# Closing waits for unawaited transfers only, and the last output chunk in two column parts

## The chip, the cores and the metric

The kernel runs on one core of a Trainium2 chip. The metric is the device time in microseconds of one execution. A profile gives the span from the first to the last instruction; in every execution of this study the time is 1.8 to 1.9 us longer than the span, whatever the kernel.

## The reference

Linear attention with a per-head RMS norm, then a residual token-mixing layer and a two-layer MLP on 8 batches of 576 x 512. Only the last lines matter here:

```python
u  = x + lam * tok
a2 = alpha2 * u + beta2
ch = np.maximum(a2 @ w_ch1, 0.0) @ w_ch2
return (u + lam * ch).astype(np.float32)
```

## The kernel before

A small scheduler in the kernel file places operations on engines and works out the waits between them. In the program a semaphore is a counter that an engine or a transfer (DMA) raises and on which another engine waits. Each DMA has a semaphore of its own; at the end SyncE waits for every one.

```python
    def emit(self):
        ...
        for o in self.sequence:
            if o.lat is not None:                      # a DMA
                val[o.idx] = (self.stack.enter_context(nc.semaphore("d%d" % o.idx)), 16)
            elif o.inc:
                count[o.eng] += 1
                val[o.idx] = (sems[o.eng], count[o.eng])
        ...
            for o in self.sequence:
                ...                                    # waits, the operation, its increment
            for o in self.sequence:
                if o.lat is not None:
                    nc.sync.wait_ge(*val[o.idx])       # the closing waits
```

The second MLP layer of batch `b` handles chunks of 128 rows in the order 0 to 4 (four in even batches). Chunk 4 holds the last 64 rows of two batches, so it needs two stores of 64 rows.

```python
        def ch2(b, pri, span):
            ...
            nch = 5 if b % 2 else 4
            def mm(c, fj, p):
                ...                                     # 16 matmuls of 128x512 into t
                P.op({"DVE": dve_us(512)}, lambda e, _: e.tensor_tensor(
                    out=lc[:], in0=t.flat(), in1=lam_bc[:], op=ALU.mult), ...)
                P.op(..., lambda e, _: e.tensor_tensor(out=x, in0=x, in1=lc[:], op=ALU.add), ...)
                if c < 4:
                    ... e.dma_start(out[b, c:512:4, :], x)
                else:
                    for i in range(2):
                        ... e.dma_start(out[b - 1 + i, 512:576, :], x[64 * i:64 * i + 64, :])
            order = ... [(c, fj) for c in range(nch) for fj in range(16)]
```

## Time and profile before

| quantity | value |
|---|---|
| time, median of the first 3 runs | 367.05 us (365.95 to 367.85) |
| span of the profiled run | 365.81 us |
| PE busy | 354.1 us (97%) |
| PE's end to the end of the span | 7.44 us |
| of that: closing waits of SyncE | 68 instructions, 361.01 to 365.49 us |

SP or SyncE is the engine that issues the stores and the closing waits (SPq in the views), DVE the vector engine, PEld PE's weight loads. First the page's rows over 40 equal slices of the span (tenths busy; PEclk is PE's granted clock):

```profile
PE   8999999999899999999999999999999999999991
PEclk9899999999999999999999999999999999999997
```

PE is busy for over 80% of every slice but the last. The chain of waits of the last 25 us (start, duration, what) shows why:

```profile
341.14 10.74 PE ps L1046 x49
351.88 0.05 issue
351.93 6.44 PE ps L1046 x29
358.37 0.02 issue
358.39 0.70 DVE lc L1054
359.09 0.02 issue
359.12 0.69 DVE xtl L1059
```

PE runs without a hole to 358.37. Then DVE multiplies and adds the last chunk. The timeline of the same stretch goes on to the two stores (each line's two figures are start and extent):

```profile
358.39 0.69 DVE L1054 TENSOR_TENSOR lc<-ps,lam_bc 128x512 f32<-128x512 f32 x1 [2.04 <-PE ps L1046]
359.12 0.69 DVE L1059 TENSOR_TENSOR xtl<-xtl,lc 128x512 f32<-128x512 f32 x1
359.84 1.12 SPq L1066 DMA_DIRECT2D out_dram<-xtl  x2
```

The stores are issued by 360.96, yet the span lasts to 365.81. Waits are not listed in the timeline; the view by source line has them. First the line of the closing waits (duration of one, then first and last start):

```profile
L403 SPq EVENT_SEMAPHORE  x68: 28/28/28, 361.0 to 365.5; - x68
```

Each is listed at 28 ns, but in the trace their starts stand 61 ns apart (the median; the last one starts 0.38 us after the one before), so 68 of them fill 4.5 us. (Each waits for two semaphores: the builder had paired the 136 waits.) A table by stage shows that nothing else happens in most of that time (columns: stretch, its length, busy time of PE, PEld, DVE, ACT, POOL, then PEclk, DMA share, GB/s):

```profile
358.40:359.84 1.44, 0.00 (x0) 0.00 (x0) 1.38 (x2) 0.00 (x0) 0.00 (x0) 1.00 0.00 0
359.84:361.00 1.16, 0.00 (x0) 0.00 (x0) 0.00 (x0) 0.00 (x0) 0.00 (x0) 1.00 0.03 7
361.00:362.75 1.75, 0.00 (x0) 0.00 (x0) 0.00 (x0) 0.00 (x0) 0.00 (x0) 0.54 0.63 145
362.75:365.50 2.75, 0.00 (x0) 0.00 (x0) 0.00 (x0) 0.00 (x0) 0.00 (x0) 0.50 0.00 0
365.50:365.82 0.32, 0.00 (x0) 0.00 (x0) 0.00 (x0) 0.00 (x0) 0.00 (x0) 0.50 0.00 0
```

The last store has landed at 362.73 (landing is the moment at which the trace records its semaphore as full). From there to 365.50 no engine and no DMA does anything: SyncE works through waits that have long been satisfied. The listed 28 ns of all 68 come to 1.9 us, not to the 4.5 us that they fill, so starts, not durations, are to be read here; what lies between the end of one and the start of the next the trace does not show.

### The profile page before, as it was taken

To read this page: it belongs to the slowest core of one execution; us is meant where nothing else is said; L and a number is where in the kernel's file an instruction comes from. 1 tells how busy PE (TensorE), PEld (TensorE's weight loads), DVE (VectorE), ACT (ScalarE), POOL (GpSimd) and SP (SyncE) were. 2 spreads that over 40 slices of the span, in tenths; PEclk is the share of its full clock that TensorE was granted. 3 is DMA by queue.
4 is the path that set the end of the run, shared out by engine and by line. 5 is a ranking of instruction groups with operands and counts; after the bars stand their busy time and mean duration, and the time that the engine had idled before them with its cause. 6 is when DMAs were issued, how large, how long until landed. Compare 5 with 4: busy or idle time off the path is not lost.

```text
span 365.8 us, 5605 instructions
## 1 busy us (share of the span) xinstructions
PE 354.1 (97%) x2177; PEld 218.6 (60%) x2206; DVE 226.2 (62%) x409; ACT 171.8 (47%) x295; POOL 118.9 (32%) x113
## 2 busy tenths in 40 slices
PE   8999999999899999999999999999999999999991
PEld 2687574678775565457855655457754544467540
DVE  3579769995895599648946572748455774410141
ACT  3579766577971387015831476017610362036200
POOL 3645014430451462045502571047402750220000
PEclk9899999999999999999999999999999999999997
DMA  6999999997859426921002120311022111310011
GB/s 184 369 389 387 339 395 276 310 364 229 288 176 244 128 59 202 231 72 59 0 16 72 58 59 0 65 66 59 0 36 80 57 30 30 86 73 0 29 59 57
DMA packets 62485, 51.53 MB, mean 141 GB/s; under 512 B 28784, under 2 KB 53368, under 8 KB 62460
## 3 DMA queue, kind: packets, MB, share of 16 engines
q1 hardware_dynamic: 62208, 51.01, 44.7%
q8 instruction: 17, 0.28, 0.3%
q10 hardware_dynamic: 252, 0.18, 0.1%
q14 instruction: 8, 0.07, 0.1%
HBM read 38.20 MB, written 9.44 MB: 130 GB/s over the span
## 4 chain that ended last, share of the span: by engine, by line
PE 89%; DVE 6%; ACT 1%; issue 1%; POOL 0%
PE ps L1026 34%; PE ps L1046 30%; PE ps L918 7%; PE ps L590 5%; PE ps L1133 4%; PE ps L608 3%; PE ps L864 1%; DVE rt L691 1%; PE ps L931 1%; DVE yn L689 1%; DVE lc L1054 1%; PE ps L835 1%; PE ps L740 1%; PE ps L1146 1%; PE ps L767 1%
## 5 line engine op out<-in xcount | busy, mean ns | idle before, releaser
L1026 PE MATMUL ps<-a2t,w 128*128 128x320 bf16 (+1 forms) x760 | 142.0, 329 | 2.0 <-ACT ht L1011 1.6
L1046 PE MATMUL ps<-w,ht 128*128 128x512 bf16 x560 | 136.3, 382 | 0.5
L1026 PEld LDWEIGHTS ps<-a2t,w 128*128 128x128 bf16 x768 | 73.3, 98 | 42.9 <-ACT ht L1011 1.8
L1046 PEld LDWEIGHTS ps<-w,ht 128*128 128x128 bf16 x576 | 54.9, 98 | 60.3 <-issue 0.2
L1011 ACT ACTIVATE ht<-ps 128x640 bf16<-128x640 f32 (+1 forms) x97 | 63.4, 654 | 53.1 <-PE ps L1026 52.8
L1059 POOL TENSOR_TENSOR xm<-xm,lc 128x512 f32<-128x512 f32 x28 | 36.3, 1298 | 121.2 <-DVE lc L1054 121.0
L1054 DVE TENSOR_TENSOR lc<-ps,lam_bc 128x512 f32<-128x512 f32 x36 | 24.9, 691 | 62.1 <-PE ps L1046 61.6
L694 POOL TENSOR_TENSOR xm<-yn,g_bc 128x512 f32<-128x512 f32 x28 | 40.9, 1462 | 45.2 <-DVE yn L689 42.9
L676 ACT ACTIVATE sq<-ps 128x512 f32<-128x512 f32 (+1 forms) x35 | 20.5, 593 | 63.2 <-PE ps L590 63.0
L923 DVE TENSOR_TENSOR xm<-ps,xm 128x512 f32<-128x512 f32 x28 | 19.2, 690 | 27.2 <-PE ps L918 25.9
L590 PE MATMUL ps<-kvc,qt 128*128 128x128 f32 x112 | 32.4, 386 | 0.0
L590 PE MATMUL ps<-identr,qr 128*128 128x128 f32 x112 | 31.1, 370 | 0.4 <-DVE yn L689 0.4
L608 PE MATMUL ps<-vr,kr 128*128 128x128 f32 (+1 forms) x112 | 29.7, 358 | 0.0
L918 PE MATMUL ps<-rt,wt 128*128 128x512 bf16 x107 | 28.3, 380 | 0.3
L678 DVE TENSOR_REDUCE small<-sq 128x8 f32<-128x512 f32 (+1 forms) x35 | 23.4, 674 | 5.8 <-ACT sq L676 5.7
L1012 DVE TENSOR_SCALAR ht<-ps 128x512 bf16<-128x512 f32 (+1 forms) x31 | 22.7, 739 | 6.7 <-PE ps L1026 6.4
L689 DVE TENSOR_TENSOR yn<-ps,small 128x512 f32<-128x512 f32 (+1 forms) x35 | 23.9, 686 | 0.7
L590 PEld LDWEIGHTS ps<-kvc,qt 128*128 128x128 f32 x112 | 22.1, 200 | 2.0 <-ACT ht L1011 0.2
L691 DVE TENSOR_TENSOR rt<-yn,ge 128x512 bf16<-128x512 f32 x24 | 22.3, 942 | 0.4
L590 PEld LDWEIGHTS ps<-identr,qr 128*128 128x128 f32 x112 | 21.5, 200 | 1.6 <-DVE yn L689 0.6
L608 PEld LDWEIGHTS ps<-vr,kr 128*128 128x128 f32 x112 | 21.6, 200 | 0.5 <-issue 0.2
L420 ACT ACTIVATE qt<-ps 128x512 fp32r<-128x512 f32 (+1 forms) x26 | 14.9, 571 | 9.8 <-PE ps L590 6.9
(152 smaller groups left out, 369.7 us busy)
## 6 DMA issues: line engine op xcount, KB each, us to landing
st<-in_moe_w_ch_dram SPq DMA_DIRECT2D x8, 1024.0 KB, 10.6
out_dram<-xm SPq DMA_DIRECT2D x32, 256.0 KB, 2.3
st<-in_q_dram SPq DMA_DIRECT2D x7, 1024.0 KB, 6.1
st<-in_k_dram SPq DMA_DIRECT2D x7, 1024.0 KB, 9.1
st<-in_v_dram SPq DMA_DIRECT2D x7, 1024.0 KB, 11.2
ht<-in_moe_w_tok_dram SPq DMA_DIRECT2D x2, 576.0 KB, 7.8
kvft<-in_k_dram SPq DMA_DIRECT2D x8, 128.0 KB, 5.9
kvft<-in_v_dram SPq DMA_DIRECT2D x8, 128.0 KB, 5.6
```

Of the source, the lines that this page charges most:

```text
L590: P.op(F, lambda e, _: e.matmul(t.flat()[:, 128 * pr:128 * pr + 128], a(), m(), start=True, stop=True), r=r, w=[t], kind="F", **kw)
L608: return e.matmul(o, a, m, start=(c == 0), stop=(c == 4))
L678: P.op({"DVE": dve_us(512)}, lambda e, _: e.tensor_reduce(out=small[rows, s4], in_=sq[rows, s2], axis=AX.X, op=ALU.add), r=[("sq", s2)], w ...
L689: P.op({"DVE": dve_us(512)}, lambda e, _: e.tensor_tensor(out=hview(yn[rows, s3, :]), in0=hview(t.flat(rows)), in1=bc, op=ALU.mult), r=[t, ...
L691: P.op({"DVE": dve_us(512), "POOL": pool_us(512)}, lambda e, _: e.tensor_tensor(out=rto, in0=yn[rows, s3, :], in1=ge1[rows, :], op=ALU.mul ...
L694: P.op({"POOL": pool_us(512)}, lambda e, _: e.tensor_tensor(out=hview(x), in0=hview(yn[rows, s3, :]), in1=g_bc[rows, None, :].to_broadcast ...
L918: P.op({"PE": 0.216}, lambda e, _, sc=sc: e.matmul(t.flat(), wt[:, sc, 128 * c:128 * c + 128], rt[:, sc, :] if sc < 4 else rtt[:], start=( ...
L1011: return e.activation(dst, src(), ACT.Relu)
L1026: return e.matmul(o, w1[:, dj, 128 * fj:128 * fj + 128], m, start=(dj == 0), stop=(dj == 3))
L1046: P.op({"PE": 0.216}, lambda e, _: e.matmul(t.flat(), ht[:, fj, 128 * c:128 * c + 128], w2[:, fj, :], start=(fj == 0), stop=(fj == 15)), r ...
L1054: o = P.op({"DVE": dve_us(512)}, lambda e, _: e.tensor_tensor(out=lc[:], in0=t.flat(), in1=lam_bc[:], op=ALU.mult), r=[t, "lam"], w=["lc"] ...
L1059: lambda e, _: e.tensor_tensor(out=x, in0=x, in1=lc[:], op=ALU.add),
```

## The change

Two things meant to shorten the tail behind PE. First, SyncE waits at the end only for transfers on which no engine has waited (the final output stores), and transfers share semaphores when the earlier one is known to be over. Second, in the last batch the chunk with two stores comes first, and the last chunk is computed, evacuated and stored as 320 and then 192 columns.

```diff
         for o in self.sequence:
             if o.lat is not None:
-                val[o.idx] = (self.stack.enter_context(nc.semaphore("d%d" % o.idx)), 16)
+                c = next((c for c in used if ("dma", c[2].idx) in o.clock), None)
+                if c is None:
+                    c = [self.stack.enter_context(nc.semaphore("d%d" % o.idx)), 0, None]
+                else:
+                    used.remove(c)
+                c[1], c[2] = c[1] + 16, o
+                used.append(c)
+                val[o.idx] = (c[0], c[1])
@@
+            awaited = set(y.idx for o in self.sequence for y in o.waits)
             for o in self.sequence:
-                if o.lat is not None:
+                if o.lat is not None and o.idx not in awaited:
                     nc.sync.wait_ge(*val[o.idx])
@@ in ch2
+            end = b == NB - 1
+            cs = [4, 0, 1, 2, 3] if end else range(nch)
+            parts = {c: [(0, 512)] for c in cs}
+            if end:
+                parts[cs[-1]] = [(0, 320), (320, 512)]
   (cut: matmul, multiply, add and store take the columns lo:hi of their part;
    the adds of the last batch are set to DVE, where all five ran before too)
```

More of the change, by code (lines that the diff above doesn't have):

```diff
@@ L380, in emit @@
         count = {e: 0 for e in self.COMPUTE}
-        val = {}
+        val, used = {}, []
         for o in self.sequence:
             if o.lat is not None:
-                val[o.idx] = (self.stack.enter_context(nc.semaphore("d%d" % o.idx)), 16)
+                c = next((c for c in used if ("dma", c[2].idx) in o.clock), None)
[6 more added lines that the diff above has]
+                val[o.idx] = (c[0], c[1])
             elif o.inc:
@@ L1038, in ch2, with mm @@
             P.tag = "ch2.%d" % b
-            tiles = {}
+            tiles, made = {}, {}
             nch = 5 if b % 2 else 4
-            def mm(c, fj, p):
-                if c not in tiles:
-                    tiles[c] = P.ptile(1)
-                t = tiles[c]
-                P.op({"PE": 0.216}, lambda e, _: e.matmul(
-                    t.flat(), ht[:, fj, 128 * c:128 * c + 128], w2[:, fj, :],
+            end = b == NB - 1
[3 more added lines that the diff above has]
+                parts[cs[-1]] = [(0, 320), (320, 512)]
+            def mm(c, part, fj, p):
+                lo, hi = part
+                if (c, part) not in tiles:
+                    tiles[c, part] = P.ptile(1)
+                t = tiles[c, part]
+                n = hi - lo
+                P.op({"PE": 0.004 + n * 0.212 / 512}, lambda e, _: e.matmul(
+                    t.flat()[:, 0:n], ht[:, fj, 128 * c:128 * c + 128], w2[:, fj, lo:hi],
                     start=(fj == 0), stop=(fj == 15)),
@@ L1051, in mm @@
                     return
-                x = xm[:, b % 2, c, :] if c < 4 else xtl[:, (b // 2) % 2, :]
+                x = (xm[:, b % 2, c, :] if c < 4 else xtl[:, (b // 2) % 2, :])[:, lo:hi]
                 keys = ([xkey(b, c)] if c < 4 else [("xt", (b // 2) % 2, i) for i in range(2)])
-                o = P.op({"DVE": dve_us(512)}, lambda e, _: e.tensor_tensor(
-                    out=lc[:], in0=t.flat(), in1=lam_bc[:], op=ALU.mult), r=[t, "lam"],
-                    w=["lc"], pri=p - 2)
+                o = P.op({"DVE": dve_us(n)}, lambda e, _: e.tensor_tensor(
+                    out=lc[:, lo:hi], in0=t.flat()[:, 0:n], in1=lam_bc[:, lo:hi], op=ALU.mult),
+                    r=[t, "lam"], w=[("lc", lo)] if lo else ["lc", ("lc", lo)], pri=p - 2)
                 o.raw.update(o.deps)
-                P.op({"POOL": pool_us(512)} if b < NB - 1 else {"POOL": pool_us(512), "DVE": dve_us(512)},
-                     lambda e, _: e.tensor_tensor(out=x, in0=x, in1=lc[:], op=ALU.add),
-                     r=["lc"] + keys, w=keys, pri=p - 2, port=True)
+                if lo:
+                    P.lastw["xlast"], P.readers["xlast"] = made[c], []
+                    keys = ["xlast"]
+                else:
+                    made[c] = [y for k in keys for y in P.lastw[k]]
+                P.op({"DVE": dve_us(n)} if end else {"POOL": pool_us(n)},
+                     lambda e, _: e.tensor_tensor(out=x, in0=x, in1=lc[:, lo:hi], op=ALU.add),
+                     r=[("lc", lo)] + keys, w=keys, pri=p - 2, port=True)
                 if c < 4:
-                    P.op({"SP": 0.8}, lambda e, _: e.dma_start(out[b, c:512:4, :], x), r=keys,
+                    P.op({"SP": 0.8}, lambda e, _: e.dma_start(out[b, c:512:4, lo:hi], x), r=keys,
                          dma_us=0.8, pri=p - 5)
@@ L1068, in mm @@
                             r=[keys[i]], dma_us=0.4, pri=p - 5)
-            order = ([(c, fj) for n in range(4) for c in range(nch) for fj in range(4 * n, 4 * n + 4)]
-                     if b == 0 else [(c, fj) for c in range(nch) for fj in range(16)])
-            for i, (c, fj) in enumerate(order):
-                mm(c, fj, pri + span * i / len(order))
+            order = ([(c, parts[c][0], fj) for n in range(4) for c in range(nch) for fj in range(4 * n, 4 * n + 4)]
+                     if b == 0 else [(c, x, fj) for c in cs for x in parts[c] for fj in range(16)])
+            for i, (c, part, fj) in enumerate(order):
+                mm(c, part, fj, pri + span * i / len(order))
         load(0, -1000)
```

## The prediction

> **What bounds the kernel now.** PE: 354.1 us busy of a span of 365.8 (busy table); the chain of waits runs on PE without a hole from 341.1 to 358.4 us. The change cannot shorten that body, only the tail behind it, in which PE is idle. From the chain, the timeline and the view of the closing wait's line:
>
> - 358.39 to 359.81: DVE, 0.692 us multiply and 0.692 us add of the last 128x512 chunk.
> - 359.84 to 360.96: SyncE issues that chunk's two stores (0.49 and 0.59 us). They land at 362.10 and 362.73, 2.27 and 2.37 us after their starts.
> - 361.01 to 365.49: SyncE runs 68 closing wait instructions, two semaphores each, for all 136 transfers, 61 ns apart, nearly all long satisfied. The last bytes have landed by 362.73: 2.76 us of pure instruction stream follow.
> - 365.49 to 365.81: closing barrier, 0.32 us.
>
> **What the change does.** The order of instructions on ACT and POOL is unchanged; on PE, DVE and SyncE it differs only in the last batch's second layer and the end. The first 341 us should be equal.
>
> 1. Waits. The built program has 7 closing waits instead of 68: 7 x 0.061 = 0.43 us from the last issue's end, over before the last landing, which now sets the end. Semaphores fall from 143 to 29; waits elsewhere keep their number, so I give this no time. -2.76 us, all on the critical path.
> 2. Last chunk in 320 + 192 columns, the two-store tail chunk moved first. PE: 16 matmuls at 0.136 (the trace's 320-column pitch) plus 16 at about 0.082 (estimate: 256 columns stand 0.109 apart, 128 stand 0.056) = 3.49 against 16 x 0.216 = 3.46: +0.03 us. DVE on the chain: from 0.42 us at 256 columns and 0.692 at 512, 192 columns cost about 0.35; two take 0.74 with their gap instead of 1.42: -0.68 us. The first part's DVE work (about 1.0 us) ends within the second part's 1.31 us of matmuls.
> 3. Last store: no longer queued 0.53 us behind another: -0.53 us. It is 98 KB of 768-byte rows; I take 2.25 us to landing: -0.1 us.
>
> [...] 256 KB took 2.3 us, 128 KB 2.27, so a smaller store buys issue time, not landing.
>
> Sum: landing at about 361.4, end of span about 361.8 instead of 365.8: **-4.0 us**, about 2.8 from waits and 1.3 from split and order.
>
> **Prediction: 363.0 us, range 361.8 to 364.4.** That is 1.1% faster: chance of faster by over 2% 0.02, within 2% 0.97, slower by over 2% 0.01.
>
> **What would show it.** Seven closing waits; the last starting within 0.1 us of the last landing; DVE's last two operations near 0.35 us; PE's end still near 358.4; last store starting near 359.2; span end 0.4 us after the last landing.
>
> **What would make it wrong.** (a) Run-to-run spread: before's three runs cover 1.9 us, half of the gain. (b) 768-byte rows landing later than 2048-byte ones, or the first part's store delaying the second: up to 0.5 us lost. (c) Time outside the span may depend on the number of semaphores; I assume not. (d) 192-column matmuls may be held by their 98 ns weight loads: +0.25 us; I doubt it, as 128-column ones run at 0.056. (e) Shared semaphores may lengthen a wait in the body.

(The sum: -2.76 + 0.03 - 0.68 - 0.53 - 0.1 = -4.04. The -0.1 rests on the landings of 2.3 and 2.27 us that the paragraph gives.)

## The result

The changed kernel took 362.98 us (median of 4 runs, 361.54 to 363.41) against 367.19 us (4 runs): ratio 0.9882, 95% interval 0.9843 to 0.9921. In a second job with 5 rounds it took 363.10 us against 367.29: 0.9876, interval 0.9851 to 0.990. A ratio is the mean time of one kernel's runs over the mean of the other's of the same rounds, so it is not quite the ratio of the medians quoted. Executions over 1.5% slower than the fastest of the same kernel are left out of the means.

The profiled span fell from 365.81 to 359.68 us, by 6.1 us, which is more than the time fell. The lines that answer to those above, first the page's slices:

```profile
PE   8999999999899999999999999999999999999996
PEclk9999999999999999999999999999999999999999
```

The chain of waits at the end:

```profile
350.31 6.48 PE ps L1063 x45
356.79 0.02 issue
356.81 0.37 DVE lc L1071
357.18 0.02 issue
357.21 0.36 DVE xm L1081
```

The timeline of the last two parts:

```profile
355.50 0.49 DVE L1071 TENSOR_TENSOR lc<-ps,lam_bc 128x320 f32<-128x320 f32 x1 [0.76 <-PE ps L1063]
356.02 0.49 DVE L1081 TENSOR_TENSOR xm<-xm,lc 128x320 f32<-128x320 f32 x1
356.81 0.36 DVE L1071 TENSOR_TENSOR lc<-ps,lam_bc 128x192 f32<-128x192 f32 x1 [0.30 <-PE ps L1063]
357.21 0.36 DVE L1081 TENSOR_TENSOR xm<-xm,lc 128x192 f32<-128x192 f32 x1
```

The closing waits by source line:

```profile
L412 SPq EVENT_SEMAPHORE  x7: 17/28/28, 358.0 to 359.4; - x7
```

And the table by stage (DVE on the last part, issue of the last store, its landing, the close):

```profile
356.80:357.57 0.77, 0.00 (x0) 0.00 (x0) 0.71 (x2) 0.00 (x0) 0.00 (x0) 1.00 0.22 83
357.59:357.93 0.34, 0.00 (x0) 0.00 (x0) 0.00 (x0) 0.00 (x0) 0.00 (x0) 1.00 0.78 283
357.95:359.37 1.42, 0.00 (x0) 0.00 (x0) 0.00 (x0) 0.00 (x0) 0.00 (x0) 1.00 0.21 69
359.40:359.68 0.28, 0.00 (x0) 0.00 (x0) 0.00 (x0) 0.00 (x0) 0.00 (x0) 0.53 0.00 0
```

The 2.75 us in which SyncE alone was at work behind the last landing are gone, apart from the close: the last wait starts at 359.38, 0.02 us after the last landing at 359.37.

PE ends at 356.79 instead of 358.37, although its program is the same up to the last batch. That difference is not the change's. In the profile of before, PE's clock is granted at 0.5 for 3.41 us, from 9.57 to 12.99 us (PEclk's 8 in the second slice); in this profile of after it is not. The first half-speed stretch differs too, which PEclk does not show because the clock's records begin only at its end: the 512-column matmuls that the program calls warm-up (line 1133 before, 1155 after) stand 427 ns apart until 6.16 us before and until 4.43 us after, then 215 to 227 ns, and in the later stretch of before 427 again. The 81st instruction on DVE, the same in both programs, starts at 49.19 us before and at 47.59 after, 1.60 us apart. From it to DVE's start on the last piece it is 309.20 and 309.23 us. So the middle of the kernel is equal to 0.03 us and the 1.6 us come from its first 49 us. What sets these stretches no run shows; that they differ from execution to execution the traces do show: of the twelve profiles seven have one stretch of 3.41 us at 0.5, starting between 8.9 and 10.4 us, and five have none, and the changed kernel had it in one profile and not in another. The seven reach that DVE instruction at 48.8 to 49.6 us, four of the five at 47.5 to 48.0. No run switched it on purpose, and it is not the whole lottery: the profile of waits_only below has no such stretch and still reaches the same DVE instruction only at 48.96 us. There ACT waits 2.1 us for a load of q, until 35.02 us, PE is then idle for 1.1 us before 36.22, and DVE's lag behind the profile of after grows from 0.11 to 1.39 us between its 66th and its 68th instruction; why that load came late I did not pursue.

To compare kernels regardless of that, I call **tail** the time from DVE's start on the last piece (0.02 us after PE's end) to the end of the span: 7.42 us before, 2.86 us after, 4.56 us less. The 4.2 us by which the medians fell include the lottery of the start.

### The profile page after: what moved, and what is told of

It reads as the page before. It is cut to its first block, busy times and chain, and to the rows that moved or that the text cites. A ratio compares the mean times of both kernels' runs of the same rounds, so it can differ in the third digit from the quotient of the medians.

```text
span 359.7 us, 5579 instructions
## 1 busy us (share of the span) xinstructions
PE 351.9 (98%) x2193; PEld 219.2 (61%) x2222; DVE 226.2 (63%) x411; ACT 171.9 (48%) x295; POOL 118.9 (33%) x113
## 4 chain that ended last, share of the span: by engine, by line
PE 88%; DVE 6%; ACT 2%; DMA 1%; issue 1%; POOL 0%; SPq 0%
PE ps L1035 35%; PE ps L1063 31%; PE ps L927 7%; PE ps L599 5%; PE ps L617 3%; PE ps L1155 2%; PE ps L873 2%; DMA kvft<-in_v_dram 1%; DVE rt L700 1%; PE ps L940 1%; DVE yn L698 1%; PE ps L844 1%; PE ps L749 1%; DVE lc L1071 1%; PE ps L776 1%
## 5 line engine op out<-in xcount | busy, mean ns | idle before, releaser
L1063 PE MATMUL ps<-w,ht 128*128 128x512 bf16 (+2 forms) x576 | 136.4, 376 | 0.5
L1063 PEld LDWEIGHTS ps<-w,ht 128*128 128x128 bf16 x592 | 56.2, 98 | 59.3 <-issue 0.2
L1071 DVE TENSOR_TENSOR lc<-ps,lam_bc 128x512 f32<-128x512 f32 (+2 forms) x37 | 25.0, 677 | 61.2 <-PE ps L1063 60.7
L927 PEld LDWEIGHTS ps<-rt,wt 128*128 128x128 bf16 x112 | 10.9, 98 | 12.5
```

What stands on the lines that cost most here:

```text
L927: P.op({"PE": 0.216}, lambda e, _, sc=sc: e.matmul(t.flat(), wt[:, sc, 128 * c:128 * c + 128], rt[:, sc, :] if sc < 4 else rtt[:], start=( ...
L1063: P.op({"PE": 0.004 + n * 0.212 / 512}, lambda e, _: e.matmul(t.flat()[:, 0:n], ht[:, fj, 128 * c:128 * c + 128], w2[:, fj, lo:hi], start= ...
L1071: o = P.op({"DVE": dve_us(n)}, lambda e, _: e.tensor_tensor(out=lc[:, lo:hi], in0=t.flat()[:, 0:n], in1=lam_bc[:, lo:hi], op=ALU.mult), r= ...
```

## The experiments

All ten runs gave correct results. The tail is read from one profile of each. This table has, for each kernel, points in its tail read from the trace's records of instructions and semaphores (us after DVE's start on the last piece), then the times. Kernels of one job share the runs of before.

| kernel | last store starts | lands | closing wait instructions: number, first, last | tail | median us | ratio to before (95%) |
|---|---|---|---|---|---|---|
| before | 1.97 | 4.34 | 68, 2.62, 7.07 | 7.42 | 367.29 (11 runs) | |
| after_again | 0.78 | 2.56 | 7, 1.16, 2.57 | 2.86 | 363.10 | 0.9876 (0.9851 to 0.9900) |
| waits_only | 1.97 | 4.34 | 6, 2.61, 4.36 | 4.64 | 364.58 | 0.9916 (0.9893 to 0.9939) |
| split_only | 0.78 | 2.52 | 69, 1.16, 5.67 | 5.97 | 365.95 | 0.9961 (0.9940 to 0.9982) |
| no_reuse | 0.78 | 2.52 | 7, 1.16, 2.54 | 2.83 | 362.93 | 0.9875 (0.9854 to 0.9897) |
| order_only | 1.45 | 3.73 | 6, 1.83, 3.75 | 4.04 | 363.94 | 0.9887 (0.9870 to 0.9903) |
| early_waits | 0.78 | 2.52 | 6, 1.15, 2.54 | 2.83 | 361.68 | 0.9839 (0.9822 to 0.9855) |
| dose_40 | 0.78 | 2.52 | 20, 1.16, 2.54 | 2.83 | 361.97 (1 run) | |
| dose_90 | 0.78 | 2.52 | 45, 1.16, 3.85 | 4.14 | 364.19 (1 run) | |
| probe_stores | 0.78 | 2.52 | 8, 1.16, 2.54 | 2.83 | 361.68 (1 run) | |
| split3 | 0.64 | 2.23 | 7, 1.03, 2.25 | 2.54 | 362.10 | 0.9850 (0.9815 to 0.9885) |

The first four after before are one job (5 rounds each), the next four another (before: 367.88), the last two a third (before: 367.33). Each job ran on another chip, so times are compared with the runs of before in the same job.

### after_again, waits_only, split_only, no_reuse: the change and its parts

after_again is the changed kernel unedited.

> The changed kernel once more, for the same chip and rounds as its halves. Call tail the time from DVE's start on the last piece (0.02 us after PE's end) to the end of the span: 7.42 us before, 2.86 us in the first profile after. Theory (the gain is the tail alone): tail 2.9 us again, time 4.6 us under before on average. Rival (the body got faster too, since the profiled span fell by 6.1 us and not by 4.6): PE ends near 356.8 us again and the time is about 6 us under before.

The tail is 2.86 us again. This time the profile has the half-clock stretch at its start, and DVE starts on the last piece at 358.49 us, as late as before (358.39). So the rival, a faster body, falls.

waits_only is the kernel before with the new closing waits and shared semaphores alone:

```diff
-    (the kernel before: emit as it was)
+    (emit of the change; ch2 as it was)
```

> The old last batch with the new closing waits and shared semaphores. Theory: the last landing, 4.34 us after DVE's start on the last chunk, ends the span 0.3 us later: tail 4.7 us, 2.75 us less than before. Rival (the closing waits were hidden under the landing of the last store): tail 7.4 us, no gain.

The tail is 4.64 us, 2.78 less than before; the last wait starts 0.02 us after the last landing. The waits were not hidden.

split_only is the reverse:

```diff
-    (the changed kernel: emit of the change)
+    (emit as it was before, a semaphore and a closing wait for each of 137 transfers)
```

> The new last batch with the old closing waits, one semaphore for each of 137 transfers. Theory: 69 wait instructions of 0.061 us start at the last issue's end (1.16 us into the tail), which is 1.4 us earlier than before: 1.16 + 4.2 + 0.3, and up to 0.35 more if the last wait hesitates as it did before: tail 5.7 to 6.0 us, 1.4 to 1.7 less than before; the early landing of the last store then earns nothing. Rival (the split and order carry the gain): tail 2.9 us.

The tail is 5.97 us. The line of its closing waits:

```profile
L403 SPq EVENT_SEMAPHORE  x69: 17/28/28, 359.2 to 363.7; - x69
```

The last store lands 1.8 us earlier than before (2.52 instead of 4.34), and this is worth only 1.45 us, namely the earlier start of the waits (1.16 instead of 2.62). As long as SyncE has 4 us of waits to run, when the store lands does not matter; only when the last issue is over. So the parts are not independent: 2.78 + 1.45 = 4.23, both together 4.56.

no_reuse keeps the filter but gives each transfer its own semaphore (144 in the program instead of 29):

```diff
-                c = next((c for c in used if ("dma", c[2].idx) in o.clock), None)
-                (cut: the rest of the sharing)
+                val[o.idx] = (self.stack.enter_context(nc.semaphore("d%d" % o.idx)), 16)
```

> The changed kernel, with a semaphore of its own for each transfer (144 instead of 29), the closing waits still filtered. Theory: reuse of semaphores is worth nothing, tail 2.9 us and the time of the changed kernel within the noise. Rival (fewer semaphores cost less at the start, in the body or outside the span): slower than the changed kernel by 0.5 us or more, or another difference of time and span than 1.9 us.

Its tail is 2.83 us, its ratio 0.9875 beside 0.9876, and time minus span is 1.87 us in the profiled run, as it is for the changed kernel (1.86 in after_again) and before (1.87). Sharing semaphores is worth nothing here that these runs could show.

### order_only: the split taken out

```diff
-                parts[cs[-1]] = [(0, 320), (320, 512)]
+                parts[cs[-1]] = [(0, 512)]
```

> New closing waits and the new order (the chunk with two stores first), but the last chunk whole: 128x512, one store of 256 KB. Theory, from the first runs: DVE 1.43 us, store starts 1.45 us into the tail and lands 2.27 us later as the 128x512 stores of before did, closing 0.3 us: tail 4.0 us, so 0.62 us of waits_only's 4.64 are the second store's place in the queue, and 1.2 us of the changed kernel's 2.86 are left to the split. Rival (the split alone is worth it, the order nothing): tail 4.6 us.

The tail is 4.04 us. Against waits_only, moving the two-store chunk forward is worth 0.60 us: the last store starts 0.52 us earlier and lands in 2.29 instead of 2.37 us. The split is worth the other 1.18: 0.67 us of DVE (store start 1.45 to 0.78) and 0.51 us of landing (2.29 to 1.78).

### early_waits, dose_40, dose_90: what a closing wait costs, and when

early_waits drops no wait. It moves all but twelve ahead of the fourth store from the end:

```diff
+                if o is stores[-4]:
+                    for y in stores[:-12]:
+                        nc.sync.wait_ge(*val[y.idx])
@@
-                if o.lat is not None and o.idx not in awaited:
+            (the closing waits: the last twelve transfers only)
```

> The new last batch, no wait dropped and one semaphore for each transfer, but the waits for all transfers except the last twelve stand ahead of the fourth store from the end, where SyncE is idle anyway; only twelve are left for the end. Theory (the place of the waits costs, not their number): tail 2.9 us as in the changed kernel, although 137 transfers are awaited; one earlier store starts up to 1 us late, off the chain. Rival (every wait costs wherever it stands): time of split_only, about 3 us over the changed kernel.

The tail is 2.83 us. The two groups of waits, by source line; first those moved forward:

```profile
L397 SPq EVENT_SEMAPHORE  x62: 17/28/28, 348.2 to 351.9; - x62
```

Then those left at the end:

```profile
L407 SPq EVENT_SEMAPHORE  x6: 28/28/28, 357.9 to 359.3; - x6
```

The 62 instructions cost what they always cost, 3.7 us, but SyncE had that time: the following store started at 352.05, 0.8 us late, and nobody waited for it. So it is the place of a wait that costs, not its number. The time, 361.68 us, looks better than the changed kernel's 363.10, but that was another job on another chip, and no run shows a merit of the kernel: none of its four runs shows the lower clock of the stretch at the start (granted clock 0.999 to 1.0), while five of the six of after_again do (0.995). The tails differ by 0.03 us.

dose_40 and dose_90 add waits back to the changed kernel (with own semaphores), to 40 and 90:

```diff
+            more = [o for o in some if o.idx in awaited][:27]      # dose_90: [:77]
-                if o.lat is not None and o.idx not in awaited:
+                if o.idx not in awaited or o in more:
```

> The changed kernel with 40 closing waits (20 instructions) and own semaphores. Theory: they start 1.16 us into the tail and take 20 x 0.061 = 1.2 us, over by 2.4 us, before the last landing at 2.54: tail 2.9 us, nothing lost. Rival (every wait adds its 0.06 us): tail 3.6 us.

The tail is 2.83 us: 20 instructions are over before the landing and cost nothing.

> The changed kernel with 90 closing waits (45 instructions) and own semaphores. Theory: 1.16 + 45 x 0.061 = 3.9 us, past the landing at 2.54, plus 0.3 for the close and up to 0.35 if the last wait hesitates as in before: tail 4.2 to 4.5 us. Rival as for dose_40: 38 more instructions than the changed kernel, tail 5.2 us.

The tail is 4.14 us; 44 steps from the first to the last wait take 2.69 us, 61 ns each. Together with the changed kernel (7 instructions, tail 2.86) and split_only (69, 5.97) this is a knee: free until the landing, (2.55 - 1.16) / 0.061 = about 23 instructions, then 61 ns each. split_only has 0.36 us on top, most of it because one of its waits stands 0.38 us behind the one before. Before and early_waits have such a gap as well, and in all three it falls on the 208th SyncE instruction in the trace. The shorter programs have no 208th. In these three profiles, and in no other, an additional 8 KB packet of the instruction queue (q14) starts 0.6 to 0.9 us after the end of the gap (in two of them just behind the end of the span); the cause of the gap I have not tested.

### probe_stores: why the store landed earlier than predicted

Three earlier stores of the last batch, off the chain, are each cut in two. The first of each pair has no other transfer ahead of it.

```diff
-                    P.op({"SP": 0.8}, lambda e, _: e.dma_start(out[b, c:512:4, lo:hi], x), ...)
+                    cuts = {0: [(0, 64, 0, 512), (64, 128, 0, 512)],
+                            1: [(0, 128, 0, 192), (0, 128, 192, 512)],
+                            2: [(0, 128, 0, 64), (0, 128, 64, 512)]}     # rows, columns
+                    for r0, r1, f0, f1 in ...: e.dma_start(out[...], x[r0:r1, f0:f1])
```

> What was mis-sized is the landing of the 192-column store: 1.74 to 1.78 us measured, 2.25 predicted, because a 64x512 store of half the bytes of a 128x512 one had landed no sooner (2.27 against 2.28). In the changed kernel three earlier stores of the last batch, off the chain and 3.45 us apart, are cut in two: 64 rows of 512 columns, then the other 64; 192 columns of 128 rows, then 320; 64 columns, then 448. The first of each pair has nothing ahead of it. Theory (landing goes with bytes: 98 KB 1.76, 164 KB 2.01, 256 KB 2.29, and the 64-row store of the tail chunk was late for another reason, its issue, 0.49 instead of 0.33 us): 128x192 at 1.76 again, 128x64 (33 KB) at about 1.5, and 64x512 (131 KB) of these rows at about 1.9, or at 2.05 with an issue of 0.49. Rival (landing goes with the length of a row): 64x512 at 2.28 like the 128x512 stores, with an issue of 0.33; 128x64 at about 1.6. Tail unchanged, 2.85.

The view of DMA issues up to 356.6 us (size of one, median us from issue to landing where the view gives it):

```profile
out_dram<-xtl SPq DMA_DIRECT2D x2, 128.0 KB, 2.3
out_dram<-xm SPq DMA_DIRECT2D x2, 128.0 KB, 2.3
...
out_dram<-xm SPq DMA_DIRECT2D x1, 96.0 KB, 1.8
out_dram<-xm SPq DMA_DIRECT2D x1, 32.0 KB, 1.5
```

The trace's packet records take the landing apart. All are stores of the last batch whose packets met no packets of an earlier store, and all times are in us from the start of the issue (KB are 1024 bytes here, 1000 in the expectation):

| store (kernel) | KB | issue us | first packet starts | one row's packet, ns | last packet ends | landed |
|---|---|---|---|---|---|---|
| 128x64 (probe_stores) | 32 | 0.33 | 0.83 | 18 | 1.10 | 1.52 |
| 128x128 (split3, last) | 64 | 0.33 | 0.83 | 27 | 1.18 | 1.59 |
| 128x192 (probe_stores, last) | 96 | 0.33 | 0.83 | 35 | 1.27 | 1.75 |
| 128x256 (split3) | 128 | 0.33 | 0.83 | 45 | 1.35 | 1.88 |
| 128x320 (probe_stores) | 160 | 0.33 | 0.84 | 54 | 1.43 | 2.01 |
| 128x512 (before) | 256 | 0.33 | 0.83 | 82 | 1.65 | 2.27 |
| 64x512 (probe_stores) | 128 | 0.47 | 1.13 | 151 | 1.89 | 2.32 |
| 64x512, tail chunk (before) | 128 | 0.49 | 1.14 | 151 | 1.91 | 2.27 |

(Behind each of the two 64-row stores follows a second one with rows of the same size. I take the end of the first from its 16 packets of 4 bytes, one set of which closes each store. The second store is not what makes the rows slow: those that start before 1.5 us, when no packet of it can be there yet, take 148 and 151 ns in the median.) Among 128-row stores the landing grows steadily with the bytes: (2.27 - 1.52) / 224 KB = 3.3 ns per KB; the rows grow with them, so these stores alone do not tell the two apart. Before their first packet pass 0.83 to 0.84 us from the start of the issue, and 0.41 to 0.62 us from the last packet's end to the landing. The 64-row store of the same kind of rows lands as late as a 128-row store of twice the bytes. Its issue is longer (0.47 us instead of 0.33), as the theory had it, but its landing of 2.32 is what the rival said. Neither was right alone: its first packet starts 0.30 us later, and each 2048-byte row takes 151 ns instead of 82. That is 1.84 times as long for a row; why a store over 64 partitions does so no run here shows.

### split3: one step further

```diff
-                parts[cs[-1]] = [(0, 320), (320, 512)]
+                parts[cs[-1]] = [(0, 256), (256, 384), (384, 512)]
```

> The changed kernel with the last chunk in three parts of 256, 128 and 128 columns. Theory: PE 16 x (0.109 + 2 x 0.056) = 3.54 instead of 3.49 us, +0.05; two DVE operations of 128 columns take 0.6 us instead of 0.75, and the 64 KB store lands in about 1.65 instead of 1.76: tail 2.6 us, 0.2 to 0.25 less than the changed kernel, too little to show in the time against run-to-run spread. Rival (the fixed part of a store is all that is left, or 128-column matmuls are held by their weight loads): tail 2.85, or PE over 3.8 us.

The timeline of its last part:

```profile
358.89 0.29 DVE L1071 TENSOR_TENSOR lc<-ps,lam_bc 128x128 f32<-128x128 f32 x1 [0.28 <-PE ps L1063]
359.21 0.29 DVE L1081 TENSOR_TENSOR xm<-xm,lc 128x128 f32<-128x128 f32 x1
```

The tail is 2.54 us, 0.32 less than the changed kernel's. From DVE's start on the chunk before it to DVE's start on the last part it is 3.53 us instead of 3.49 (before: 3.45), and the starts of before's matmuls, 109 ns apart at 256 columns and 56 at 128, make 16 x (0.109 + 2 x 0.056) = 3.54, so these matmuls of 128 columns show no hold by their weight loads (98 ns each). The net gain is 0.28 us. It is the shortest chain, but the times (median 362.10, four runs) do not show it: the gain is smaller than the lottery of the start.

## Why the prediction was right, and where a term was off

Predicted 363.0 us, measured 362.98 and 363.10. The terms:

| term of the sum | predicted | measured |
|---|---|---|
| closing waits behind the last landing | -2.76 | -2.78 (waits_only against before) |
| second store no longer in the queue | -0.53 | -0.52 (order_only against waits_only, store start) |
| DVE on 192 columns instead of 512 | -0.68 | -0.67 (store start, split against order_only) |
| landing of the last store | -0.1 | -0.59 (0.08 from the order, 0.51 from the size) |
| PE, extra matmuls | +0.03 | +0.04 (3.49 against 3.45 us) |
| sum | -4.0 | -4.5 |

- **Right:** what bounds the tail, the cost per closing wait (61 ns), its full place on the chain, and that sharing semaphores earned nothing (ratio 0.9876 with, 0.9875 without). waits_only, no_reuse and the doses show these.
- **Mis-sized:** the landing of the last store. The prediction took "2.25 us to landing: -0.1 us", from "256 KB took 2.3 us, 128 KB 2.27, so a smaller store buys issue time, not landing". It landed in 1.78 us. The step that failed was the comparison: the 128 KB store covered only 64 partitions, and at 64 partitions a row takes 151 ns instead of 82 and the first packet starts 0.3 us later. Two differences had cancelled, and I read the result as "size does not matter". A 128-row store of 128 KB lands in 1.88 us. Nor does a smaller store buy issue time: it was 0.33 to 0.34 us at every size from 32 to 256 KB over 128 rows, and 0.47 to 0.59 us for 128 KB over 64.
- **Right with some luck:** the gain was about 0.5 us larger than the sum. That the median still hit shows no more than that the runs of each kernel spread over about 2 us (the prediction's point (a)), which hides 0.5. The profiled span, 359.7 instead of the predicted 361.8, was off by 2.1 us: 0.5 from the landing and 1.6 from the start.
- **Points (b), (d) and (e) of what could go wrong** did not occur: shorter rows landed sooner (1.78 us for 768 bytes, 2.27 for 2048), 192-column matmuls stood 82 ns apart as estimated, and the body kept its length to 0.03 us. Point (c) did not either (no_reuse: time minus span 1.87 us with 144 semaphores).

## What to carry to other kernels

When the profile shows time after the last landing with no engine and no DMA busy, look at the waits of the issuing engine: here an instruction that waits for satisfied semaphores took 61 ns from start to start, so the 68 behind the last store filled 4.5 us. Such waits were free where that engine was idle (62 in early_waits) or where they ended before the last landing (20 in dose_40; tail 2.83 us in both). Make the last piece small in all its stages, with one store over all 128 partitions at the end (128 KB landed in 1.88 us from 128 rows, in 2.32 us from 64); before sizing a transfer from another one, check that both cover the same partitions. Where the gain is below the run-to-run spread, compare the stretch of the trace that the change can touch, not the span.
